# Sums of squares of two weight matrices: from Gram products on TensorE to squares on ScalarE

## The chip, the cores and the metric

The kernel runs on one core of one Trainium2 chip. The core has five engines with instruction streams of their own: PE (TensorE, matrix products), DVE (VectorE), ACT (ScalarE), POOL (GpSimd) and SP (SyncE, which issues the loads and stores here). What counts is the time of one execution in microseconds (us); the median of several runs is compared.

## The reference

Local and pooled attention feeds a mixing layer with an MLP (first block of weights), and then a gated layer. Cut to what matters here:

```python
def _moe_ref(x, w_ch1, w_ch2):               # x (4, 576, 512), w_ch1 (512, 2048), w_ch2 (2048, 512)
    X = np.fft.fft(np.fft.fft(x, axis=1), axis=2)
    u = x + np.real(X).astype(np.float32)
    mu = np.mean(u, axis=-1, keepdims=True)
    var = np.mean((u - mu) ** 2, axis=-1, keepdims=True)
    un = (u - mu) / np.sqrt(var + 1e-06)
    ch = np.maximum(un @ w_ch1, 0.0) @ w_ch2
    return (u + ch).astype(np.float32)

x = attention(q, k, v)                       # local window of 4, plus attention over means of 4
y = _moe_ref(x, w_ch1, w_ch2)
out = (sigmoid(conv5(y, conv_w)) * (y @ w_val)) @ w_out
```

## The kernel before

The inputs arrive as 64-bit floats. W1 (`w_ch1`, 512x2048) and W2 (`w_ch2`, 2048x512) are loaded as 32-bit halves of them, in eight tiles each, and DVE turns each tile of 128x1024 into float32 "words" by three instructions of `to_f32`: one shift (L302) and two instructions with two tensor inputs (L166, the helper `stt`). W1's tiles are taken in the order `W1_ORDER`; their places in that order are called positions 0 to 7. W2's tiles are 8 to 15.

The MLP works on 12 units of 192 positions, (b, j) for batch b and j = 0 to 2. Unit (0, 0) multiplies the float32 words themselves (`steps32`: the products `ph` with W1 at L1068, `pc` with W2 at L1081). This is the "coarse" unit. All other units multiply a float16 high and low part, in three passes (`mlp_steps`: `ph` at L1106, `pc` at L1126, with `hh` and `hl` the two parts of the hidden layer). For these "fine" units each weight tile is scaled by a power of two and split: `conv_w` lets ACT write the high part (L372) and DVE the low part (L166, float16 out). A tile's high part is put where the words of the tile before it stood, so the tiles of W1 are split one behind the other, ACT and DVE in turn.

The power of two comes from the sum of all squares of the matrix. `sumsq_w` forms it by Gram products: eight 128x128 bf16 products a tile (L356), 64 for W1 and 64 for W2, all added in one PSUM tile. `diagonal` multiplies this by the identity and reduces it (DVE), `total` adds over partitions with one more product (`tot`), ACT scales the result (`f2s_w1`, `f2s_w2`, L258), and `pow2` makes `s_w1` or `s_w2` and its inverse by four small instructions on POOL (L244 to L248). The split of W1 waits for `s_w1`, that of W2 for `s_w2`.

The norm in front of unit (b, j) is `ln`: mean, difference (`u32` for unit (0, 0), `uc` for the others), squares by ACT, their sum on PE (`st`), and an inverse root. For the units (0, 0) and (0, 1) the root is made on POOL by nine instructions on 128x192 (L1012, L169, L1019), with results `r00` and `r0`. `r00` is used only at the end of the coarse unit. `r0` is waited for by DVE's `uc<-uc,r` (L169), which the fine unit (0, 1) needs.

The order of the work is set by positions: `put` and `spread` give each step a number, the steps are emitted in the order of these numbers, `urgent` and `issue_after` (through the helper `behind`) add priorities and "not before" edges, and a scheduler then orders each engine's instructions. Loads stand in one chain on SP.

## Time and profile before

| what | value |
|---|---|
| median of 3 runs | 729.0 us (728.07 to 730.03) |
| the profiled execution | 730.66 us, of which the span is 728.9 us |
| PE busy | 687.0 us (94%) |
| DVE busy | 467.0 us (64%) |
| ACT busy | 316.9 us (43%) |
| POOL busy | 122.5 us (17%) |
| mean granted TensorE clock | 0.967 |

The span reaches from the first to the last instruction of the profiled execution; 1.7 us of its time lie outside it. A busy share over the whole span says little for one stretch: the stages have different limits, so the stretches around the change are read apart.

### The profile page before, as it was taken

Reading aid. Unit: us, or ns where it says so; the run is one execution under the profiler, and the core shown is the slowest. Engines: PE = TensorE matmul, PEld = TensorE weight load, DVE = VectorE, ACT = ScalarE, POOL = GpSimd, SP = SyncE. Lnnn points to the kernel's source line nnn. Section 1 sums busy time; section 2 is a strip of 40 time slices with the busy share of each in tenths; the row PEclk is TensorE's granted clock in tenths of the full one; section 3 lists DMA queues with packets and bytes.
Section 4 is the critical chain, followed back from the end, with each engine's and each line's share of the span. In section 5 each row is a group of like instructions: output and inputs, shape, how many; then the busy total and the mean of one; then the engine's idle time right before and its main releaser. Section 6 shows DMA issues by size and latency. Waiting matters only on the chain.

```text
span 728.9 us, 18440 instructions
## 1 busy us (share of the span) xinstructions
PE 687.0 (94%) x7849; PEld 599.6 (82%) x7849; DVE 467.0 (64%) x978; ACT 316.9 (43%) x980; POOL 122.5 (17%) x167
## 2 busy tenths in 40 slices
PE   8588799989899988999999999999999999999997
PEld 4346599988778967868898898789899989999895
DVE  4885699987978776466976725829635572633324
ACT  1674224686355336756423835644413232322212
POOL 0400054025222022330202107003100010000000
PEclk9758999989999999999999999999999999999999
DMA  9964314623422301240230001003000000000001
GB/s 240 377 228 167 101 66 167 155 82 129 144 60 83 100 1 39 61 136 16 77 103 2 26 15 43 17 1 97 18 16 16 1 16 16 1 17 2 30 2 44
DMA packets 27574, 53.01 MB, mean 73 GB/s; under 512 B 2112, under 2 KB 16320, under 8 KB 26468
## 3 DMA queue, kind: packets, MB, share of 16 engines
q1 hardware_dynamic: 27492, 51.84, 22.1%
q8 instruction: 61, 1.00, 0.6%
q14 instruction: 21, 0.17, 0.1%
HBM read 45.34 MB, written 8.26 MB: 74 GB/s over the span
## 4 chain that ended last, share of the span: by engine, by line
PE 67%; DVE 18%; ACT 6%; DMA 5%; POOL 2%; issue 1%; SPq 1%; POOLq 0%; ACTq 0%; DVEq 0%
PE pc L1126 19%; PE ph L1106 18%; DVE W L166 6%; PE out L1234 5%; PE val L1218 5%; ACT dP L565 3%; DMA v<-in_v_dram 2%; PE po L751 2%; PE ab L863 1%; DVE fF L835 1%; PE dO L606 1%; PE ph L1068 1%; DVE X L172 1%; PE sc L701 1%; PE pc L1081 1%
## 5 line engine op out<-in xcount | busy, mean ns | idle before, releaser
L1106 PE MATMUL ph<-uh,W 128*128 128x192 f16 x1408 | 195.3, 246 | 1.6 <-ACT uh L1032 1.6
L1106 PEld LDWEIGHTS <-W 128*128 128x128 f16 x2112 | 175.1, 98 | 7.9 <-issue 6.4
L1106 PE MATMUL ph<-ul,W 128*128 128x192 f16 x704 | 173.2, 246 | 0.0
L1126 PE MATMUL pc<-hh,W 128*128 128x192 f16 x1232 | 171.6, 247 | 0.9 <-ACT hh L1110 0.9
L1126 PEld LDWEIGHTS <-W 128*128 128x128 f16 x1848 | 154.2, 98 | 10.4 <-issue 8.4
L1126 PE MATMUL pc<-hl,W 128*128 128x192 f16 x616 | 151.3, 247 | 3.9 <-DVE hl L166 3.9
L166 DVE SCALAR_TENSOR_TENSOR hl<-ph,hh 128x384 f16<-128x384 f32 x88 | 48.2, 550 | 91.3 <-ACT hh L1110 91.2
L1110 ACT ACTIVATE hh<-ph 128x384 f16<-128x384 f32 x88 | 43.1, 494 | 103.0 <-PE ph L1106 99.9
L166 DVE SCALAR_TENSOR_TENSOR W<-X,cw,W 128x192 f32<-128x192 f32 x160 | 60.2, 432 | 0.9 <-ACT W L1181 0.7
L1218 PE MATMUL val<-yy,W 128*128 128x192 f16 x576 | 52.9, 246 | 0.1
L1218 PEld LDWEIGHTS <-W 128*128 128x128 f16 x576 | 47.9, 98 | 2.4 <-issue 0.6
L565 ACT ACTIVATE dP<-dS,dmx 128x64 f32<-128x64 f32 x160 | 48.1, 337 | 0.7 <-PE dPT L586 0.3
L1234 PE MATMUL out<-W,gh 128*128 128x512 f16 x144 | 45.6, 379 | 0.0
L565 ACT ACTIVATION_READ_ACCUMULATOR dP<-dS,dmx 128x1 f32 x160 | 36.8, 230 | 0.0
L166 DVE SCALAR_TENSOR_TENSOR W<-W,W 128x1024 int32<-128x1024 int32 x24 | 29.0, 1232 | 0.1
L715 ACT ACTIVATE E<-sc,nm 72x144 f32<-72x144 f32 x64 | 23.6, 378 | 9.4 <-POOL vr L172 4.7
L1234 PE MATMUL out<-W,gl 128*128 128x512 f16 x72 | 27.3, 379 | 0.0
L1081 PE MATMUL pc<-h,W 128*128 128x192 f32 x128 | 26.2, 357 | 0.0
L1234 PEld LDWEIGHTS <-gh 128*128 128x128 f16 x144 | 14.1, 98 | 13.7 <-issue 0.2
L1126 PE MATMUL pc<-hh,Wz 128*128 128x192 f16 x176 | 25.2, 246 | 0.0
L1068 PE MATMUL ph<-u,W 128*128 128x192 f32 x128 | 24.0, 345 | 1.0 <-DVE u L996 1.0
L1126 PEld LDWEIGHTS <-Wz 128*128 128x128 f16 x264 | 22.2, 98 | 2.7 <-issue 0.2
(243 smaller groups left out, 1208.1 us busy)
## 6 DMA issues: line engine op xcount, KB each, us to landing
W<-in_moe_w_ch_dram SPq DMA_DIRECT2D x12, 1024.0 KB
v<-in_v_dram SPq DMA_DIRECT2D x32, 144.0 KB
out_dram<-osb SPq DMA_DIRECT2D x17, 256.0 KB
vw<-in_v_dram SPq DMA_DIRECT2D x16, 256.0 KB
X<-in_q_dram SPq DMA_DIRECT2D x6, 576.0 KB
kT<-in_k_dram SPq DMA_DIRECT2D x4, 582.0 KB
X<-in_moe_w_ch_dram SPq DMA_DIRECT2D x2, 1024.0 KB
raw<-in_moe_w_ch_dram SPq DMA_DIRECT2D x4, 512.0 KB
```

Source lines behind the costliest of these rows:

```text
L166: return eng.scalar_tensor_tensor(out=out, in0=in0, scalar=scalar, in1=in1, op0=op0, op1=op1)
L172: return eng.tensor_tensor(out=out, in0=a, in1=b, op=ALU.add)
L565: A.activation(out=s_[:, z, a], in_=pss[par][:, z, a], func=AF.Exp, scale=SCALE, bias=mx[:, par, z, a:a + 1], accum_out=su[:, par, z, a:a ...
L715: A.activation(out=E[:, qc], in_=ps[:, qc], func=AF.Exp, scale=SCALE / 16, bias=nm[:, qc:qc + 1], accum_out=su[:, qc:qc + 1],)
L751: T.matmul(out=po[par * 64:par * 64 + 64], lhsT=d["vr"][:, kc, (a % 2) * 4 + (a // 2) * 2 + par], rhs=ets[par][:, kc], start=(kc == 0), st ...
L1068: i = T.matmul(out=ps[:, e], lhsT=W[AT[kc * 2 + m // 8] + 1][:, o:o + 128], rhs=u()[:, kc, :], start=(kc == 0), stop=(kc == 3))
L1081: T.matmul(out=c["ps"][m // 2][:, m % 2], lhsT=W[9 + g][:, o:o + 128], rhs=hs[g // 2][:, g % 2, e, :], start=(kk == 0 and m % 2 == 0), sto ...
L1106: T.matmul(out=ps[:, e], lhsT=w1_ap(pw, kc, 2 * g + e), rhs=uh[px][:, kc, :], start=(t == 0), stop=(t == 11))
L1110: A.activation(out=h_, in_=ps, func=AF.Relu)
L1126: T.matmul(out=ps[m // 2][:, m % 2], lhsT=w2_ap(pw, kk, m), rhs=x[px][:, e, :], start=(kk == 0 and (pw, px) == (0, 0) and m % 2 == 0), sto ...
L1218: T.matmul(out=ps[:, e], lhsT=wv_ap(pw, kc, 2 * mh + e), rhs=m_["y"][px][:, kc, :], start=(t == 0), stop=(t == 11))
L1234: T.matmul(out=ps, lhsT=(gh, gl)[px][:, kc, t * 128:(t + 1) * 128], rhs=wo_ap(pw, kc), start=(n == 0), stop=(n == 11))
```

## The change

Three things change. The sums of squares of W1 and W2 are made by ACT: one square of each 128x1024 tile with an accumulated sum, into one of eight columns, with the squares themselves thrown into a scratch tile (`Wz`). The Gram products and the diagonal go for these two (the third weight, `w_out`, keeps them), and `tot` now has eight columns, which ACT adds while it scales. The words of W1's tiles at positions 6 and 7 move from a place behind the first norm to the group of the other W1 tiles. The root of norm (0, 0) is emitted behind W1's scale, with an edge that keeps it there.

```diff
-S_W1B = -7.47
@@ pow2
         for dst, sg, z in ((s, 1.0, 0.0), (iv, -1.0, 254.0)):
-            eng.tensor_scalar(out=dst.bitcast(I32), in0=e, scalar1=sg * 2.0 ** 23, scalar2=z * 2.0 ** 23, op0=ALU.mult, op1=ALU.add)
+            last = eng.tensor_scalar(out=dst.bitcast(I32), in0=e, scalar1=sg * 2.0 ** 23, scalar2=z * 2.0 ** 23, op0=ALU.mult, op1=ALU.add)
+        if name == "w1":
+            st[0]["scaled"] = last
@@ total
         if act:
-            assert n == 1
             r = keep.tile([P, 1], F32, name="f2s_" + name)
-            A.activation(out=r, in_=ps, func=AF.Copy, scale=float(DM))
+            A.activation(out=tiny.tile([P, n], F32, tag="p2t", name="p2t"), in_=ps, func=AF.Copy, scale=float(DM), accum_out=r)
             return r
@@ word_w
-                       lambda g=gates if pos < 4 else gates1 if pos < 6 else gates2: g.pop(0) if len(g) > 1 else g[0])
-            if pos == 7:
-                gates2[:] = [last.ins]
+                       lambda g=gates if pos < 4 else gates1 if pos < 8 else gates2: g.pop(0) if len(g) > 1 else g[0])
@@ sumsq_w
+        if key != "wo":
+            if first:
+                gram[key] = keep.tile([P, 8], F32, name="ss_" + key)
+            behind(st[0]["sq"].ins if i < 8 else None, lambda: A.activation(
+                out=spare.bitcast(BF16)[:, 0:1024], in_=W[AT[i] + 1], func=AF.Square,
+                accum_out=gram[key][:, i % 8:i % 8 + 1]))
+            return
         if first:
-            gram[key] = pst("cv", [P, P]) if key == "wo" else ps_c.tile([P, P], F32, tag="c1", name="gram")
+            gram[key] = pst("cv", [P, P])
         x = W[AT[i] + 1].bitcast(BF16).rearrange("p (n t) -> p n t", t=2)
         for c in range(8):
             blk = x[:, c * 128:(c + 1) * 128, 1]
-            behind(st[0]["st2"].ins if i < 8 else None, lambda: T.matmul(
-                out=gram[key], lhsT=blk, rhs=blk, start=(first and c == 0), stop=(last and c == 7)))
+            T.matmul(out=gram[key], lhsT=blk, rhs=blk, start=(first and c == 0), stop=(last and c == 7))
@@ trace_w
-        return total(diagonal(gram[key], key), 1, key, key in ("w1", "w2"))
+        if key == "wo":
+            return total(diagonal(gram[key], key), 1, key)
+        return total(gram[key], 8, key, True)
@@ ln
+        def root():
+            behind(st[0]["scaled"].ins if head else None, lambda: e.tensor_scalar(out=r0.bitcast(I32), ...))
...
+        if head:
+            st[0]["r"], st[0]["root"] = r0, root
+            return
+        root()
@@ the positions
     put(S_G1[1], lambda: urgent(w1_scale, "S"))
+    put(S_G1[1], lambda: st[0]["root"]())
...
-    for r, f, p in ((W1_ORDER[:6], w_in, S_W1), ...
+    for r, f, p in ((W1_ORDER, w_in, S_W1), ...
-    for i in W1_ORDER[6:]:
-        put(S_W1B, lambda i=i: urgent(lambda: w_in(i), "S"))
```

The edits move instructions on all engines. Three places carry the prediction.

The first is POOL, at the two roots and W1's scale. `p2a`, `p2b`, `s_w1` and `iv_w1` are W1's scale, `r00` and one `r1` belong to the root of norm (0, 0), `r0` and the other `r1` to that of norm (0, 1). Before (the end of the second root; the whole first root and half of the second stand ahead of these rows):

```order
L169 TENSOR_TENSOR r1_1302<-r0_1300 128x192
L169 TENSOR_TENSOR r1_1302<-r1_1302,vv_1298 128x192
L244 TENSOR_SCALAR p2a_1207<-f2s_w1_1203 128x1
L1019 TENSOR_SCALAR r1_1302<-r1_1302 128x192
L246 TENSOR_SCALAR p2b_1209<-p2a_1207 128x1
L169 TENSOR_TENSOR r0_1300<-r0_1300,r1_1302 128x192
L248 TENSOR_SCALAR s_w1_1205<-p2b_1209 128x1
L248 TENSOR_SCALAR iv_w1_1206<-p2b_1209 128x1
```

Now:

```order
L243 TENSOR_SCALAR p2a_1139<-f2s_w1_1134 128x1
L245 TENSOR_SCALAR p2b_1141<-p2a_1139 128x1
L247 TENSOR_SCALAR s_w1_1137<-p2b_1141 128x1
L247 TENSOR_SCALAR iv_w1_1138<-p2b_1141 128x1
L1023 TENSOR_SCALAR r00_1083<-vv_1081 128x192
L168 TENSOR_TENSOR r1_1084<-r00_1083 128x192
L1023 TENSOR_SCALAR r0_1241<-vv_1239 128x192
L168 TENSOR_TENSOR r1_1084<-r1_1084,vv_1081 128x192
L168 TENSOR_TENSOR r1_1242<-r0_1241 128x192
L1029 TENSOR_SCALAR r1_1084<-r1_1084 128x192
...
L1029 TENSOR_SCALAR r1_1242<-r1_1242 128x192
L168 TENSOR_TENSOR r0_1241<-r0_1241,r1_1242 128x192
```

The scale stood behind 16 of the 18 instructions of the roots; now it stands ahead of all 18, the two roots alternate, and the last instruction of them is the one that DVE waits for.

The second place is ACT, from the square of the first norm to W1's scale and its first split. `Wz,ss_w1` and `Wz,ss_w2` are the new squares, `h32` the coarse unit's hidden layer, `vv` the norms' variances. Before:

```order
L1002 ACTIVATE sq_1068<-u32_1061 128x768
L1072 ACTIVATE h32_1213<-ph_1214 128x384
L1008 ACTIVATE vv_1075<-st_1070 128x192
L1002 ACTIVATE sq_1291<-uc_1284 128x768
...
L1008 ACTIVATE vv_1298<-st_1293 128x192
...
L258 ACTIVATE f2s_w1_1203<-tot_1201 128x1
L372 ACTIVATE W0_124<-W1_114,s_w1_1205 128x1024
```

Now:

```order
L1083 ACTIVATE h32_1154<-ph_1215 128x384
L352 ACTIVATE Wz_127,ss_w1_1123<-W7_117 128x1024
L1008 ACTIVATE sq_1232<-uc_1225 128x768
L352 ACTIVATE Wz_127,ss_w2_1341<-W9_118 128x1024
L1083 ACTIVATE h32_1257<-ph_1258 128x384
L352 ACTIVATE Wz_127,ss_w2_1341<-W9_118 128x1024
L352 ACTIVATE Wz_127,ss_w2_1341<-W11_119 128x1024
L258 ACTIVATE p2t_1135,f2s_w1_1134<-tot_1132 128x8
L352 ACTIVATE Wz_127,ss_w2_1341<-W11_119 128x1024
L1016 ACTIVATE vv_1239<-st_1234 128x192
L378 ACTIVATE W0_124<-W1_114,s_w1_1137 128x1024
```

All eight squares of W1 now stand between the square of norm (0, 0) and that of norm (0, 1), and three squares of W2 between the latter and W1's scale.

The third place is DVE, behind the difference of the first norm (`u32`). Before, there and at the place where DVE takes up the root's result:

```order
L996 TENSOR_TENSOR u32_1061<-X_132,st_1062 128x768
L302 TENSOR_SCALAR W7_117<-W13_120 128x1024
L302 TENSOR_SCALAR W7_117<-W15_121 128x1024
L166 SCALAR_TENSOR_TENSOR W7_117<-W13_120,W7_117 128x1024
...
L302 TENSOR_SCALAR W9_118<-W17_122 128x1024
L302 TENSOR_SCALAR W9_118<-W19_123 128x1024
...
L619 TENSOR_REDUCE qkT_805<-X_126 128x288 x2
L302 TENSOR_SCALAR W13_120<-W19_123 128x1024
L169 TENSOR_TENSOR uc_1284<-uc_1284,r0_1300 128x768
```

Now, at the same two places:

```order
L1002 TENSOR_TENSOR u32_1067<-X_132,st_1068 128x768
L302 TENSOR_SCALAR W9_118<-W17_122 128x1024
L302 TENSOR_SCALAR W9_118<-W19_123 128x1024
...
L625 TENSOR_REDUCE qkT_811<-X_126 128x288 x2
...
L165 SCALAR_TENSOR_TENSOR W13_120<-W19_123,W13_120 128x1024
L168 TENSOR_TENSOR uc_1225<-uc_1225,r0_1241 128x768
L165 SCALAR_TENSOR_TENSOR W13_120<-raw_1105,W13_120 128x512
...
L575 RECIPROCAL dsu_1197<-dsu_1197 128x8
L560 TENSOR_REDUCE dmx_1304<-dS_1268 128x8
```

The six instructions on `W7` have gone from here to the group that works on `W5`, in front of the first mixing steps. Between the reductions `qkT` and `uc<-uc,r0` stood one shift; now fifteen rows stand between them, and the `dmx` of the next attention group is still behind it.

## Rows read from the trace of the kernel before

**Rows 1.** Windows: stretch and its length, busy us of each engine, granted clock, DMA share, GB/s.

```profile
core 0: us, PE busy (x) PEld busy (x) DVE busy (x) ACT busy (x) POOL busy (x), PEclk, DMA share, GB/s
91.00:151.00 60.00, 59.43 (x621) 56.88 (x621) 59.22 (x83) 26.58 (x82) 20.59 (x28) 0.97 0.41 122
151.00:161.00 10.00, 7.80 (x47) 7.41 (x47) 7.77 (x10) 9.97 (x35) 0.00 (x0) 0.66 0.36 120
161.00:187.00 26.00, 21.87 (x312) 19.68 (x309) 21.34 (x39) 15.19 (x39) 13.99 (x13) 1.00 0.34 110
187.00:728.90 541.90, 527.86 (x6218) 472.32 (x6216) 320.78 (x734) 223.08 (x646) 77.79 (x105) 1.00 0.12 39
```

**Rows 2.** Chain of work that ended last, 90 to 187 us: start, length, what.

```profile
99.96 3.67 PE gram L356 x64
...
171.74 3.16 POOL vr L172
...
176.94 4.54 DMA raw<-in_moe_w_val_dram
```

**Rows 3.** Page, costliest groups: the attention's exponentials (busy, mean ns, idle before).

```profile
L565 ACT ACTIVATE dP<-dS,dmx 128x64 f32<-128x64 f32 x160 | 48.1, 337 | 0.7 <-PE dPT L586 0.3
```

**Rows 4.** Timeline of DVE, 90 to 135 us: start, busy, instruction, idle before.

```profile
91.38 1.29 DVE L302 TENSOR_SCALAR W<-W 128x1024 int32<-128x1024 int32 x2
92.58 4.62 DVE L166 SCALAR_TENSOR_TENSOR W<-W,W 128x1024 int32<-128x1024 int32 x4
...
109.62 1.10 DVE L302 TENSOR_SCALAR W<-W 128x1024 int32<-128x1024 int32 x1
...
113.37 5.12 DVE L619 TENSOR_REDUCE qkT<-X 128x288 f32<-128x1152 f32 x4
...
133.41 1.23 DVE L554 TENSOR_REDUCE dmx<-dS 128x8 f32<-128x512 f32 x2
```

**Rows 5.** Timeline of DVE, 50 to 66 us: the gap ahead of the mixing steps.

```profile
64.69 1.43 DVE L172 TENSOR_TENSOR X<-X,base 128x576 f32<-128x576 f32 x2 [8.67 <-ACT X L612]
```

**Rows 6.** Windows, the first 56 us.

```profile
0.00:56.00 56.00, 41.41 (x354) 23.45 (x355) 38.95 (x77) 30.39 (x155) 9.79 (x15) 0.74 0.85 282
```

**Rows 7.** Timeline of SP: the loads of W2's next tiles.

```profile
104.58 1.90 SPq L187 DMA_DIRECT2D W<-in_moe_w_ch_dram  x2
```

**Rows 8.** Timeline of ACT: the two scales, and the first split behind each.

```profile
111.98 0.17 ACT L258 ACTIVATE f2s_w<-tot 128x1 f32<-128x1 f32 x1
117.89 1.15 ACT L372 ACTIVATE W<-W,s_w 128x1024 f16<-128x1024 f32 x1 [5.74 <-POOL s_w L248]
...
150.53 1.15 ACT L372 ACTIVATE Wz<-W,s_w 128x1024 f16<-128x1024 f32 x1 [2.08 <-POOL s_w L248]
```

**Rows 9.** Timeline of ACT: a square with a sum of 128x1024 elsewhere in the kernel.

```profile
173.05 1.06 ACT L614 ACTIVATE vw<-vw 128x1024 f32<-128x1024 f32 x1
173.99 0.20 ACT L614 ACTIVATION_READ_ACCUMULATOR vw<-vw 128x1 f32 x1
```

**Rows 10.** Timeline of POOL: first, third, twelfth and sixteenth instruction of the two roots.

```profile
99.12 1.31 POOL L1012 TENSOR_SCALAR r<-vv 128x192 int32<-128x192 int32 x1 [17.63 <-ACT vv L1008]
...
101.10 3.91 POOL L169 TENSOR_TENSOR r<-r,vv 128x192 f32<-128x192 f32 x1
...
112.44 1.46 POOL L169 TENSOR_TENSOR r<-r,vv 128x192 f32<-128x192 f32 x1
...
115.67 0.59 POOL L169 TENSOR_TENSOR r<-r,vv 128x192 f32<-128x192 f32 x1
```

**Rows 11.** Timeline of PE, 103 to 167 us: coarse products, a gap, and the first fine `pc`.

```profile
103.47 3.47 PE L1068 MATMUL ph<-u,W 128*128 128x192 f32 x20
...
153.25 1.11 PE L606 MATMUL dO<-PT,vw 64*64 64x58 f32 x16 [2.20 <-ACT PT L592]
154.29 6.55 PE L1081 MATMUL pc<-h,W 128*128 128x192 f32 x22
...
166.47 0.25 PE L1126 MATMUL pc<-hh,Wz 128*128 128x192 f16 x1
```

More of the change, by code (lines that the diff above doesn't have):

```diff
@@ L1001, in ln @@
         sq = l_t("sq", [P, 4, UT])
-        A.activation(out=sq, in_=uc, func=AF.Square)
+        i = A.activation(out=sq, in_=uc, func=AF.Square)
+        if head:
+            st[0]["sq"] = i
         ps = colsum(sq, sq)
@@ L1011, in ln @@
         r0 = keep.tile([P, UT], F32, name="r00") if head else tiny.tile([P, UT], F32, tag="r0", name="r0", bufs=2)
-        e.tensor_scalar(out=r0.bitcast(I32), in0=vv.bitcast(I32), scalar1=-0.5, scalar2=float(0x5F1FFFF9),
-                        op0=ALU.mult, op1=ALU.add)
         r1 = tiny.tile([P, UT], F32, tag="r1", name="r1", bufs=2)
-        for a, c in ((-0.703952253, 0.703952253 * 2.38924456), (-0.5, 1.5)):
-            mul(e, r1, r0, r0)
-            if e is G:
-                mul(e, r1, r1, vv)
-                e.tensor_scalar(out=r1, in0=r1, scalar1=a, scalar2=c, op0=ALU.mult, op1=ALU.add)
-                mul(e, r0, r0, r1)
-            else:
-                stt(e, r1, r1, a, vv, ALU.mult, ALU.mult)
-                stt(e, r0, r1, c, r0, ALU.add, ALU.mult)
+        def root():
+            behind(st[0]["scaled"].ins if head else None, lambda: e.tensor_scalar(out=r0.bitcast(I32), in0=vv.bitcast(I32), scalar1=-0.5, scalar2=float(0x5F1FFFF9),
+                op0=ALU.mult, op1=ALU.add))
+            for a, c in ((-0.703952253, 0.703952253 * 2.38924456), (-0.5, 1.5)):
+                mul(e, r1, r0, r0)
+                if e is G:
+                    mul(e, r1, r1, vv)
+                    e.tensor_scalar(out=r1, in0=r1, scalar1=a, scalar2=c, op0=ALU.mult, op1=ALU.add)
+                    mul(e, r0, r0, r1)
+                else:
+                    stt(e, r1, r1, a, vv, ALU.mult, ALU.mult)
+                    stt(e, r0, r1, c, r0, ALU.add, ALU.mult)
+        if head:
+            st[0]["r"], st[0]["root"] = r0, root
+            return
+        root()
         r1 = r0
-        if head:
-            st[0]["r"] = r1
-            return
         mul(V, uc, uc, r1.unsqueeze(1).to_broadcast([P, 4, UT]))
@@ L1348, in attn_moe_kernel @@
         spread(steps, *p)
-    for r, f, p in ((W1_ORDER[:6], w_in, S_W1), (W1_ORDER[:4], w_out_, S_C0), (W1_ORDER[4:], w_out_, S_C1), (range(8, 16), w_in2, S_W2)):
+    for r, f, p in ((W1_ORDER, w_in, S_W1), (W1_ORDER[:4], w_out_, S_C0), (W1_ORDER[4:], w_out_, S_C1), (range(8, 16), w_in2, S_W2)):
         spread([(1.0, lambda i=i, f=f: urgent(lambda: f(i), "W")) for i in r], *p)
-    for i in W1_ORDER[6:]:
-        put(S_W1B, lambda i=i: urgent(lambda: w_in(i), "S"))
     for i in range(8, 16):
@@ L1361, in attn_moe_kernel @@
     assert S_LD[1] <= S_T0[0] and S_L1 <= S_W1[0] and S_T0[1] <= S_S0[0] and S_S0[1] <= S_F0[0] and S_F0[1] <= S_N0
-    assert S_N0 < S_W1B <= S_W2[0] and 4 / 17 < S_C0[0] and 8 / 17 < S_C1[0] and S_C1[1] <= 9 / 17
+    assert S_N0 <= S_W2[0] and 4 / 17 < S_C0[0] and 8 / 17 < S_C1[0] and S_C1[1] <= 9 / 17
     assert S_S0[1] <= S_END <= S_F0[0] and 1 <= S_W3[0]
```

## The prediction

> **What bounds the kernel now.** I read the windows first. Between 91 and 151 us, where the coarse unit runs and the weights are prepared, both PE (59.43 us) and DVE (59.22 us) are busy for the whole 60 us; ACT has 26.58 and POOL 20.59 [rows 1]. So two engines bound this stretch together, and work taken from only one of them would be worth little. From 151 to 187 us PE has holes: 2.2 us in the ten us behind 151, with the granted clock at 0.66 there, and 4.1 us up to 187. Behind 187 PE is busy for 527.86 of 541.90 us: the rest of the kernel is PE's, and whatever lead there is at 187 is carried to the end. The question is thus how much earlier the state of 187 us is reached.
>
> The chain of waits ends this stretch with an item that is not PE's: POOL's `vr` at 171.74, then the load of `w_val`, 4.54 us from 176.94 [rows 2], whose words DVE makes ahead of a low part `hl` that PE waits for. Both loads and `vr` hang on the attention of batch 1, that is on DVE's reductions `dmx`. The timeline of PE shows the hole of 2.20 us at 153.25, and behind it 22 coarse matmul pairs in 6.55 us, 0.30 each, where 20 took 3.47 us (0.17) at full clock [rows 11]. A hole on PE costs here about twice: itself, and the slower products behind it.
>
> **The Gram products.** The 64 of W1 hold the chain for 3.67 us [rows 2], so W1's and W2's together are 7.3 us of PE. It all lies in the bound stretch. PE gains from it only what DVE and ACT let it: the coarse products wait for words, and PE must turn over the attention's `dP`, which comes behind `dmx` on DVE. I count DVE's path, with PE's 7.3 us as the upper bound of a gain from this edit alone, and nothing as the lower.
>
> **The words.** The two tiles' six instructions stand on DVE from 91.38 to 97.12 us, 5.74 us [rows 4]. In the new order they go into the group in front of the mixing step, where DVE stands idle for 8.67 us until 64.69, waiting for ACT [rows 5]. They need their raw data there by about 56 us. In the first 56 us the DMA queues moved 282 GB/s, 15.8 MB [rows 6], and W1's eight tiles of 1.05 MB with the 4.9 MB ahead of them in the chain are 13.3 MB, so it has landed. 5.74 of 8.67 us: the words are hidden at no cost, with 2.9 us to spare. If the cover failed, 2.9 us or less of them would come back.
>
> So DVE leaves 91.4 us with W2's words at once. A second thing comes late by it: W2's tile 11. Its load was issued at 104.58 [rows 7], when the first words of W2 had freed its place, and used at 109.62 [rows 4], five us later. DVE now frees the place some 6.5 us earlier, at about 98.1, the load lands at 103.1, and DVE comes to it at 101.3: a wait of 1.8 us that was hidden before. The diagonal's multiplication and reduction also leave DVE, about 0.6 us as two small instructions. DVE without any other wait is thus 5.7 + 0.6 − 1.8 = 4.5 us earlier at `dmx` (133.41, [rows 4]).
>
> **The squares.** A square with a sum over 128x1024 took 1.06 us, and its sum's read ended 1.14 us behind its start [rows 9]. Sixteen are 18 us of ACT, which had 33 us idle in 91 to 151. The eight of W1 begin behind the first norm's square (about 92.4) and with `h32` and `vv` between them end at about 104; `sq` of norm (0, 1), three squares of W2 and a hidden layer follow, so `f2s_w1` comes at about 109 instead of 111.98, and as POOL's four small instructions are first in line, `s_w1` at about 110. Before, the first split began at 117.89, having waited 5.74 us for POOL [rows 8]. So W1's split is ready 8 us earlier, and ACT works it off earlier too.
>
> **The roots.** This is where the change pays. POOL used the time from 99.12 on for the roots, beside the wait for the sums; now all 18 instructions start at about 110.3. Their price depends on what DVE does: from 99.12 to 113.90 twelve took 14.8 us, 1.23 each, while DVE ran words, and a single one 3.91; under `qkT` one takes 0.59 [rows 10]. Both bounds: 18 × 0.59 = 10.6 us, end at 121; 18 × 1.23 = 22.2 us, end at 132.5. DVE takes up `r0` in `uc<-uc,r0`: `qkT` now runs from 106.7 to 111.7, and the fifteen rows behind it sum to 11 us by the durations of their kinds (four words of two inputs take 4.62), so DVE is there at about 122.8. Up to then POOL has done 2 instructions under `qkT`, some 4 in the 2.7 us of DVE's one-input rows, and 7 beside the 8.4 us of two-input rows: 13. The other 5 run while DVE stands still, at 0.6 each: DVE waits 3 us, until about 126. Everything behind `uc` on DVE waits with it, and `dmx` and `dP` of the next attention group are there.
>
> The Trainium skill says of this ("SBUF — State Buffer", section "SBUF: two separate sides") that a VectorE instruction with two SBUF inputs and a GpSimd instruction that reads SBUF take a shared port pair by an exclusive lock, and that the loser fully blocks. The trace's 3.91 us beside 0.59 agrees with it, and it speaks against moving POOL's root into DVE's words; taken strictly, it is the rival D below.
>
> **Behind `dmx`.** Of both signs: W2's diagonal, its reduction and waits are gone and a square is added, about −2; in ACT's new order the splits of W2 and sixteen exponentials (337 ns each, partly overlapping, [rows 3]) stand ahead of the first `hh` of unit (0, 1), as all its `ph` now come behind the coarse products, about +2 for the first fine `pc` (166.47, [rows 11]); the transposes of the second group, which PE had between, come earlier, about −1. Together −1, with bounds of −3 and +2.
>
> **The sum.** −4.5 + 3 − 1 = −2.5 us at 187, and PE carries it to the end. The profiled execution took 730.66 us, 1.7 above the median; the sum against it is 728.2, and against the median of 729.0, which I forecast, 726.5 us. A difference of 0.3%, 2.2 us, is about what this measurement can tell from none.
>
> **Rivals.**
> B: the root is in time (POOL near 0.59 an instruction, or `uc` reached late), and DVE and PE both gain. For it: the lower bound of 121 us lies ahead of DVE's 122.8. Then −4.5 − 1 = −5.5, and up to −7.3 where PE's own saving counts: 723.5 to 721.7 us; if the hole at 151 goes with it, down to 719.
> C: the lead at `dmx` is given back behind it. PE idles where it idled before, at 153 and up to 187, because `vr`, the load of `w_val` (4.54 us whatever the rest) and the first `hh` set it. For it: PE's 6.3 us of holes between 151 and 187 show that PE is not the limit there; against it: these loads hang on the same DVE chain, and come earlier with it. About 729.
> D, the other side: POOL is blocked by DVE's words all along and while waiting has no rest. At 1.23 us an instruction the root ends at 132.5, DVE waits 9.7 us, and −4.5 + 9.7 − 1 = +4.2: 733.2 us. It decides from a wait of about 5.5 us on, that is from a root that ends behind 128.3. Against it: while DVE waits for the root it runs nothing that could block POOL, so the last instructions are cheap.
> That the change doesn't do what it says is no rival: the Gram products and the rows of the words have moved in the new order.
>
> **Chances.** The forecast 0.42 (its own range 725 to 728; 0.27 of it faster by over 0.3%, 0.15 within), B 0.24, C 0.16, D 0.18. Faster 0.51, same 0.31, slower 0.18. The range reaches from 720 (most of B) to 732 (half of D): about 0.1 is left out on each side.
>
> **What would show it.** Right: no `gram` on PE for W1 and W2; two tiles' words between 56 and 62 us, and the next mixing step still at about 64.7; `s_w1` at about 110; POOL's last root instruction at 125 to 127, with DVE idle about 3 us ahead of `uc<-uc,r0`, released by POOL; `dmx` at about 132; the first PE hole at 151 smaller or 2 to 3 us earlier; a wait of about 2 us for the load of tile 11. Wrong: POOL's root ending behind 128 (D), or ahead of DVE (B); the mixing step later than 64.7, if the words are not covered; a lead at 133 that is gone at 187 (C); ACT late for `h32`, if PE waits for hidden layers behind the squares between 92 and 109.

## The result, and the profile after

The changed kernel takes 735.31 us (731.49 to 736.06, six executions), the kernel before on the same chip 728.16 us (727.64 to 730.03, six): a ratio of 1.0086, 95% interval 1.0063 to 1.011. It is slower by 7.1 us. The forecast was 726.5 us with a range of 720 to 732: wrong in sign, and outside the range. The profiled execution took 734.93 us, of which the span is 733.1.

The windows of the changed kernel, in the stretches of [rows 1]:

```profile
core 0: us, PE busy (x) PEld busy (x) DVE busy (x) ACT busy (x) POOL busy (x), PEclk, DMA share, GB/s
91.00:151.00 60.00, 55.97 (x533) 53.36 (x537) 54.32 (x67) 46.70 (x121) 18.74 (x28) 0.97 0.46 141
151.00:161.00 10.00, 8.53 (x98) 7.34 (x89) 7.75 (x13) 10.00 (x43) 2.27 (x3) 0.66 0.03 9
161.00:187.00 26.00, 20.42 (x268) 17.99 (x267) 24.46 (x50) 14.62 (x38) 11.04 (x10) 1.00 0.38 130
187.00:733.10 546.10, 529.12 (x6180) 471.76 (x6180) 321.86 (x725) 220.47 (x636) 81.75 (x105) 0.99 0.12 38
```

In the first row the change did what it says: PE and DVE are 3.5 and 4.9 us less busy, ACT 20 more. The rows up to 187 us have fixed ends, so the 4.2 us by which this span is longer must stand in the last row, which holds no edited instruction. I cut that row at the first fine `ph` of unit (1, 0). Before:

```profile
187.00:278.00 91.00, 85.07 (x976) 74.07 (x975) 72.60 (x167) 39.94 (x110) 17.23 (x24) 0.98 0.24 75
278.00:729.00 451.00, 442.79 (x5245) 398.25 (x5242) 248.19 (x568) 183.14 (x537) 60.55 (x81) 1.00 0.10 32
```

Changed:

```profile
187.00:281.00 94.00, 85.04 (x931) 71.20 (x932) 70.05 (x159) 38.39 (x115) 20.35 (x24) 0.95 0.20 64
281.00:733.10 452.10, 444.08 (x5251) 400.56 (x5248) 251.81 (x567) 182.07 (x522) 61.40 (x81) 1.00 0.10 33
```

The second part is 1.1 us longer; the first, with the same 85 us of PE, takes 94 instead of 91.

I then went down the path of batch 1 behind its attention, by the starts of five events: the reversal of half an image in DRAM (`dr<-dx`), the load of the result (`X<-dr`), the beginning of the norm of unit (1, 0) (`uc<-X` on DVE), the first fine `ph` of that unit on PE, and the end of the span. Two executions of either kernel (the second ones are experiments e13 and e15); every number is the start of a row of its timeline:

```
                              before  again   changed  again
dr<-dx issued (SP)            226.62  224.04  223.19   226.07
X<-dr issued (SP)             236.96  234.33  236.15   239.04
norm (1, 0) begins (DVE)      265.77  263.71  265.60   268.48
first fine ph of (1, 0) (PE)  277.62  275.68  280.77   283.65
end of the span               728.9   727.0   733.1    735.5
```

The times differ between executions by 3 us, the steps hardly. From `dr` to `X<-dr`: 10.34 and 10.29 before, 12.96 and 12.97 changed. From there to the norm: 28.81 and 29.38, 29.45 and 29.44. The norm's chain up to `ph`: 11.85 and 11.97 before, 15.17 twice changed. From `ph` to the end: 451.3 twice, and 452.3 and 451.9. By the means of the two executions the changed kernel is 0.7 us ahead at `dr`, loses 2.65 + 0.35 up to the norm, 3.26 in it, and 0.8 behind it: 6.4 us, which is the difference of the two spans' means.

These events are not PE's. PE's own time, up to `dr` and from there to the norm, before:

```profile
0.00:226.62 226.62, 198.79 (x2028) 160.67 (x2029) 177.25 (x326) 111.23 (x388) 52.00 (x70) 0.89 0.49 158
226.62:265.77 39.15, 37.78 (x454) 35.81 (x452) 30.52 (x65) 16.32 (x34) 7.11 (x12) 1.00 0.20 62
```

Changed:

```profile
0.00:223.19 223.19, 187.92 (x1866) 149.37 (x1867) 176.62 (x319) 128.26 (x422) 52.15 (x70) 0.89 0.49 160
223.19:265.60 42.41, 41.43 (x491) 38.77 (x488) 33.04 (x67) 16.26 (x34) 7.40 (x12) 1.00 0.18 57
```

Up to `dr` PE is idle for 27.83 us before and 35.27 changed (28.35 and 36.35 in the second executions): 7.7 us more in the mean, while the 128 Gram products are gone. From `dr` to the norm it is idle for 1.37 us before and 0.98 changed, though that step is 3 us longer: PE has 37 products more to do there. So `dr` now comes at an earlier point of PE's work, and a lead at `dr` is no lead in that work. When the norm begins, PE has begun 2351 products before and 2354 changed (Gram products not counted), and the changed kernel is there 2.3 us late in the mean of the two executions.

**The first loss.** The waits of SP for `X<-dr`, changed (who waited for what: us in total, times, longest):

```profile
SPq L856 <- DMA dr<-dx: 9.6, 1, 9.6
...
SPq L856 <- POOL fs L833: 2.6, 1, 2.6
```

Before, `X<-dr` waited for its transfer alone (9.6 us too). Now the transfer has landed, and it waits for POOL, whose difference `fs` still reads the part of X that the load overwrites. The timelines of POOL, before and changed:

```profile
229.20 1.92 POOL L827 TENSOR_TENSOR fs<-X 128x577 f32<-128x577 f32 x1 [6.12 <-DVE s_wo L248]
231.88 1.57 POOL L827 TENSOR_TENSOR fs<-X 128x577 f32<-128x577 f32 x1 [0.77 <-DVE ivvo L169]
```

```profile
229.85 2.37 POOL L833 TENSOR_TENSOR fs<-X 128x577 f32<-128x577 f32 x1 [9.66 <-DVE sof L165]
234.71 1.41 POOL L833 TENSOR_TENSOR fs<-X 128x577 f32<-128x577 f32 x1 [2.49 <-DVE FL L165]
```

The second ends at 236.12, and `X<-dr` is issued at 236.15. It waits for a buffer that DVE's low part `FL` gives back. DVE in the changed kernel, from the second of two splits of W_out on:

```profile
229.67 1.28 DVE L165 SCALAR_TENSOR_TENSOR W<-W,s_wo,W 128x1024 f16<-128x1024 f32 x1
230.87 1.97 DVE L165 SCALAR_TENSOR_TENSOR FL<-fF,s_x,FH 128x578 f16<-128x578 f32 x1
...
233.76 0.80 DVE L165 SCALAR_TENSOR_TENSOR FL<-fF,s_x,FH 128x578 f16<-128x578 f32 x1
```

Before, both `FL` come first (the second is shown) and the two splits of W_out follow:

```profile
230.72 1.01 DVE L166 SCALAR_TENSOR_TENSOR FL<-fF,s_x,FH 128x578 f16<-128x578 f32 x1
...
233.69 1.27 DVE L166 SCALAR_TENSOR_TENSOR W<-W,s_wo,W 128x1024 f16<-128x1024 f32 x1
```

The engines' orders are made anew with every build, and here one turned, 80 us behind the last instruction that was edited (W2's scale, whose first split stands at 144.87 us). That this costs time at the end is not shown by it: PE idles no longer here than before, as its own time above says.

**The second loss.** ACT at the norm of unit (1, 0), before:

```profile
268.39 0.84 ACT L1002 ACTIVATE sq<-uc 128x768 f32<-128x768 f32 x1 [5.34 <-DVE uc L996]
269.14 0.19 ACT L557 ACTIVATE dmx<-dmx 128x8 f32<-128x8 f32 x1
```

and changed:

```profile
267.65 0.21 ACT L563 ACTIVATE dmx<-dmx 128x8 f32<-128x8 f32 x1 [4.76 <-DVE dmx L560]
...
270.22 0.88 ACT L1008 ACTIVATE sq<-uc 128x768 f32<-128x768 f32 x1
```

The scaling `dmx` and eight exponentials of batch 2 now stand ahead of the square, on which everything hangs: `st`, the root, `uh`, and the unit's products. PE runs out of work meanwhile. Its timeline there, changed:

```profile
269.24 0.38 PE L539 MATMUL dS<-bandb 128*128 128x512 bf16 x1 [1.63 <-ACT dP L571]
...
272.81 0.98 PE L996 MATMUL st<-sq,ones 128*128 128x192 f32 x2 [1.19 <-DVE sq L171]
...
274.35 0.61 PE L1245 MATMUL out<-W,gh 128*128 128x512 f16 x1
```

Before, the same `st` stands at 270.55 and takes 0.56 us, and an `out` product 0.38: behind these holes the clock is the lower one, 1.2 GHz, in the changed kernel. The windows say it too, changed:

```profile
265.00:272.00 7.00, 3.67 (x94) 2.33 (x91) 5.19 (x11) 3.41 (x18) 1.29 (x3) 0.98 0.01 2
272.00:278.00 6.00, 5.19 (x27) 2.34 (x28) 4.69 (x9) 0.92 (x6) 2.04 (x3) 0.50 0.00 0
```

where before's second row has 1.00. So two theories: (T1) the loss is the turned orders, and undoing an order returns its part; (T2) one of the three edits costs by itself (the squares on ACT, say, or the late root), and the orders are a by-product; and as a third (T3), the lower clock is the cost. In the expectations below, theory 3 is the late root, which here is a part of T2, and T3 stands there as the second half of theory 1.

### The profile page after: what moved, and what is told of

It is laid out like the page before. It is cut to its first block, busy times and chain, and to the rows that moved or that the text cites. A ratio compares the mean times of both kernels' runs of the same rounds, so it can differ in the third digit from the quotient of the medians.

```text
span 733.1 us, 18217 instructions
## 1 busy us (share of the span) xinstructions
PE 683.5 (93%) x7721; PEld 593.5 (81%) x7721; DVE 472.8 (64%) x974; ACT 333.8 (46%) x1014; POOL 124.0 (17%) x167
## 5 line engine op out<-in xcount | busy, mean ns | idle before, releaser
L1117 PE MATMUL ph<-uh,W 128*128 128x192 f16 x1408 | 199.3, 249 | 0.6 <-ACT uh L1043 0.6
L1117 PE MATMUL ph<-ul,W 128*128 128x192 f16 x704 | 175.1, 249 | 0.7 <-DVE ul L1044 0.7
L165 DVE SCALAR_TENSOR_TENSOR W<-X,cw,W 128x192 f32<-128x192 f32 x160 | 62.8, 448 | 0.6 <-ACT W L1192 0.4
L1245 PE MATMUL out<-W,gh 128*128 128x512 f16 x144 | 47.2, 391 | 0.0
L707 PE MATMUL sc<-qkT 64*72 64x144 f32 x128 | 21.0, 326 | 3.6 <-ACT E L721 1.7
```

The source lines that it names most:

```text
L165: return eng.scalar_tensor_tensor(out=out, in0=in0, scalar=scalar, in1=in1, op0=op0, op1=op1)
L707: T.matmul(out=pss[par][:, qc], lhsT=d["qkT"][r, 0, a, qc * QC:(qc + 1) * QC], rhs=d["qkT"][r, 1, a, :], start=True, stop=True,)
L1117: T.matmul(out=ps[:, e], lhsT=w1_ap(pw, kc, 2 * g + e), rhs=uh[px][:, kc, :], start=(t == 0), stop=(t == 11))
L1245: T.matmul(out=ps, lhsT=(gh, gl)[px][:, kc, t * 128:(t + 1) * 128], rhs=wo_ap(pw, kc), start=(n == 0), stop=(n == 11))
```

## The experiments

All but the two second looks were timed in rounds against the kernel before on the same chip (medians 728.1 to 729.0 there). The groups ran on different chips, so kernels of different groups are compared by their ratios to it. None leaves out a part of the reference's computation.

### One edit at a time: e1, e2, e3, e4

e1 makes only the squares, e2 only the words, e3 only the late root, e4 squares and words with the root at its old place.

Against before, e1, e2 and e3 in this order:

```diff
+            behind(st[0]["sq"].ins if i < 8 else None, lambda: A.activation(
+                out=spare.bitcast(BF16)[:, 0:1024], in_=W[AT[i] + 1], func=AF.Square, ...
```

```diff
-    for r, f, p in ((W1_ORDER[:6], w_in, S_W1), ...
+    for r, f, p in ((W1_ORDER, w_in, S_W1), ...
```

```diff
+    put(S_G1[1], lambda: st[0]["root"]())
```

e4 against the changed kernel:

```diff
-    put(S_G1[1], lambda: st[0]["root"]())
```

> Before with the squares on ScalarE alone: words and root where they were. Theory 1 (the 7.3 us of Gram products are given back as waits on PE ahead of 187 us, and the loss of some 4 us comes from the stretch of 260 to 290 us, where the squares of the norm of unit (1, 0) now stand behind eight to sixteen exponentials on ScalarE): the order of ScalarE is turned there too, so 731 to 735 us. Theory 2 (the loss comes from what the edits do themselves between 91 and 187 us, through ScalarE's 18 us of squares): 733 to 737. Theory 3 (the root behind the scale costs the time): the root is as before, so 726 to 729.

> Before with the words of W1's tiles 6 and 7 in the first part alone; Gram products and root as they were. Theory 1: the 5.7 us go from VectorE into an idle stretch, but the order of ScalarE is turned at unit (1, 0) here too (the square behind twelve exponentials), so no better than before, 728 to 733 us. Theory 2: nothing of the squares is here, so the words' gain stays, 724 to 727 us. Theory 3: the same, 724 to 727.

> Before with the first norm's root behind W1's scale alone; Gram products and words as they were. Theory 1: the scale comes only some 2 us earlier, the root is late for VectorE by 5 us or more, and ScalarE's order is turned at unit (1, 0) too: 731 to 737 us. Theory 2: about 729. Theory 3: 733 to 737, nearly all of the loss.

> The changed kernel with the first norm's root at its old place; every other instruction stands in the changed kernel's order (TensorE's order is the same instruction for instruction). Theory 1: the wait for the root was half a us, and the late stretch is as in the changed kernel: 733 to 736 us. Theory 2: the same, 733 to 736. Theory 3: 726 to 729.

Measured: e1 735.92 us, 1.0107 [1.0075, 1.0138]; e2 731.33, 1.004 [1.0024, 1.0056]; e3 741.2, 1.0164 [1.0132, 1.0196]; e4 732.7, 1.0053 [1.0034, 1.0073]. No theory foretold all four: e1 lies above theory 1's range and in theory 2's, e2 in theory 1's alone, e3 above every range, e4 just below those of theories 1 and 2. No sum of effects explains them: e1 and e2 would make 11 us together and make 4.4, and the root that costs 13 us alone costs 2.6 in company. That speaks against T2 as a plain sum and for something that flips. The norm's chain flips: 14.55, 15.46, 14.79 and 15.17 us in e1 to e4, by the same two events as in the table. The first loss is in none of the single edits (`X<-dr` comes 10.1 to 10.2 us behind `dr` in e1 to e3), and in e4 it is (12.96).

### The order alone: e5, and back: e6, e7, e8

e5 is the kernel before with one order turned by hand, in the norm of unit (1, 0); its orders are before's until about 265 us.

```diff
-        A.activation(out=sq, in_=uc, func=AF.Square)
+        behind(st[2]["exp", 0].ins if (b, j) == (1, 0) else None, lambda: A.activation(out=sq, ...))
```

e6, e7 and e8 turn it the other way in the changed kernel, in e3 and in e1; for that the norm is also emitted at an earlier position, `P_L`.

```diff
-P_L = {1: 2.1, 2: 4.9, 3: 8.5}
+P_L = {1: 1.99, 2: 4.9, 3: 8.5}
-                A.activation(out=mx, in_=mx, func=AF.Copy, scale=-SCALE)
+                behind(st[1]["lsq"].ins if b == 2 and g == 0 else None, lambda: A.activation(out=mx, ...))
```

> The kernel before with one edge: the square of the norm of unit (1, 0) on ScalarE comes behind the eight exponentials per half of the next attention group. Up to that place, at about 265 us, every engine's order is that of before; none of the change's edits is in it. Theory 1 (the loss comes from this order, in the stretch of 260 to 290 us): 731.5 to 733.5 us. Theory 2 (the loss comes from the edits' own work between 91 and 187 us, and the late stretch only passes it on): 727.5 to 729.

> The changed kernel with one edge the other way: the next group's maximum and exponentials on ScalarE come behind the square of the norm of unit (1, 0), as in the kernel before. Theory 1: the loss behind 260 us is gone, and the 0.4 us of lead there is left: 727 to 729.5 us. Theory 2: 733 to 736, as without the edge.

> The root behind the scale alone (the slowest of the single edits, 741 us), with the same edge. Theory 1: most of its loss lies behind 260 us, where it had a lead of 2.5 us: 725 to 730 us. Theory 2: 737 to 741.

> The squares on ScalarE alone, with the same edge. Theory 1: its lead of 1.8 us at 260 us is left: 725 to 729 us. Theory 2: 733 to 736.

Measured: e5 735.03 us, 1.0086 [1.0052, 1.0119]; e6 731.81, 1.0043 [1.0026, 1.0059]; e7 730.98, 1.0028 [1.0009, 1.0047]; e8 738.06, 1.0131 [1.0103, 1.016]. One turned order, with no edit of the change in the kernel, costs 6.5 us, nearly as much as the whole loss. Up to 268 us every engine's order in e5 is before's; behind it PE's and DVE's orders turn too. ACT in e5:

```profile
268.87 0.21 ACT L557 ACTIVATE dmx<-dmx 128x8 f32<-128x8 f32 x1 [6.00 <-DVE dmx L554]
...
271.44 0.88 ACT L1002 ACTIVATE sq<-uc 128x768 f32<-128x768 f32 x1
```

Its norm begins at 265.58, as before's, and its `ph` stands at 282.17: a chain of 16.59 us, 1.4 longer than the changed kernel's, so e5 costs more than this place costs there. Turned back, the chain is 13.11 in e6 and 13.12 in e7, not before's 11.9, and 3.5 and 10.2 us come back, 3.1 and 9.9 by the ratios (6.3 of the 10.2 behind `ph`, where e3 had 457.7 us left and e7 has 451.3). Both end above the range of theory 1 and below that of theory 2. e8 is a miss, above both: its chain is 14.91, and its norm begins only at 270.69, as `dr` is issued at 230.82, 3.8 us later than in e1, whose orders are the same up to 268 us. PE waits longer on the way; in e1 this wait is 0.3 us:

```profile
PE eT L749 <- POOL E L169: 2.9, 1, 2.9
```

The `E` that PE waits for there took POOL 3.95 us, in e1 0.95 us; the part on the prediction comes back to it. So for the squares alone one order was not the cause, and what it is was not settled.

### The clock: e9, e10

Into e6 and e7 go 14 idle products of 128x512 on PE behind the first sum of that norm, so that PE does not stand still; nothing reads them.

```diff
-            T.matmul(out=ps, lhsT=ones, rhs=t[:, 0], start=True, stop=True)
+            m = T.matmul(out=ps, lhsT=ones, rhs=t[:, 0], start=True, stop=True)
+            if (b, j) == (1, 0) and src is x:
+                warm_after(m, 14)
```

> The changed kernel with the square of the norm of unit (1, 0) kept in front (as in the pinned one), and with 14 idle products of 128x512 on TensorE between the two sums of that norm, where TensorE stood idle for 3.4 us and the granted clock then fell to 0.5 for 6.8 us. Their results are not read. If what is left of the loss there is the clock (theory 1, second half): the fall goes, some 3 us are won against the pinned kernel's 731.8: 727.5 to 730. If the clock costs nothing there because TensorE waits anyway: 731 to 733.

> The root behind the scale alone, pinned, with the same 14 idle products. It came to 260 us with the best lead of all, 3.2 us, and lost it by a hole of 5.3 us and a fall of the clock. Theory 1: 726 to 729 us against 731 without the products. If the clock costs nothing there: 730 to 732.

Measured: e9 732.17 us, 1.0039 [1.0015, 1.0063]; e10 731.62, 1.0032 [1.0014, 1.005]. The windows of e9 in the same two stretches:

```profile
265.00:272.00 7.00, 6.49 (x77) 4.35 (x75) 6.06 (x12) 1.29 (x5) 1.66 (x2) 1.00 0.01 2
272.00:278.00 6.00, 5.49 (x87) 3.22 (x86) 5.01 (x13) 3.65 (x17) 2.89 (x4) 1.00 0.10 37
```

The lower clock is gone (e6 had 0.79 and 0.68 in these rows), the chain is 0.6 us shorter than in e6, and the time is the same. So T3 falls for e6: in that stretch PE waits for the chain whatever its clock. e10 says less: its clock still falls for 3.4 us there (0.76 in the first row), its chain is 13.66 us for 13.12 in e7, and its time is e7's. The products were not put into the changed kernel as it is.

### Words, Gram products and root, each with the order turned back: e11, e12, e14

e11 is e2 with e6's edit. e12 is e6 with all 128 Gram products back on PE, into a tile that nobody reads. e14 is e6 with the root at its old place; PE's order is the same in both.

The edits of e12 and of e14:

```diff
+            blk = x[:, c * 128:(c + 1) * 128, 1]
+            behind(st[0]["st2"].ins if i < 8 else None, lambda: T.matmul(
+                out=gram[key, 0], lhsT=blk, rhs=blk, start=(first and c == 0), stop=(last and c == 7)))
```

```diff
-    put(S_G1[1], lambda: st[0]["root"]())
```

> The words alone (731.3 us), with the square of the norm of unit (1, 0) kept in front of the exponentials, of which twelve of sixteen stood ahead of it. Theory 1: its lead of 0.5 us at 260 us is left: 727 to 729.5. Theory 2: 730.5 to 732.

> The changed kernel, pinned, with all 128 Gram products back on TensorE; nobody reads them, the squares of ScalarE are used. This puts 7.3 us of TensorE's work back between 100 and 150 us. If TensorE waits for the others ahead of 187 us anyway (theory 1, first half: the removed products were worth nothing): 730 to 733 us, as without them. If they were worth their length: 737 to 740.

> The changed kernel with the root of norm (0, 0) at its old place, pinned at the norm of unit (1, 0). TensorE's order is that of the pinned changed kernel, instruction for instruction. If the late root is what is left of the loss (theory 3 in part): 728 to 730 us. If not: 731 to 733.

Measured: e11 727.99 us, 0.9993 [0.9976, 1.001]; e12 732.33, 1.0046 [1.0029, 1.0064]; e14 729.73, 1.0012 [0.9993, 1.0031]. The words alone cost nothing and bring nothing; the 3 us of e2 were the order. The Gram products make no difference at the end, though they do on the way: with them PE waits, among others,

```profile
PE gram L360 <- DVE W L165: 4.5, 1, 4.5
```

and `dr` comes at 227.01 instead of 223.52. But e12's order has `X<-dr` 10.05 us behind it, and 449.8 from `ph` to the end: what the products cost, other places of its order give. So the value of the edit by itself cannot be read from this pair. The late root costs 2.1 us (e6 over e14; 2.3 by the ratios, whose intervals still overlap), of which the next pair shows the place.

### Second looks: e13, e15

e13 is the kernel before and e15 the changed one, unedited, profiled again.

> The kernel before once more, for a second profile: 727 to 731 us. If its executions differ by TensorE's clock, the falls of the clock lie at other places or are fewer than in the first profile (6.8 us from 153 and 3.4 us from 187); if they differ by waits, the clock's falls are the same.

> The changed kernel once more, for a second profile: 731 to 737 us. By theory 1 TensorE's clock falls again between 265 and 290 us, behind the holes of the norm of unit (1, 0), in most executions; if the first profile was a rare one there, it does not.

Measured: 728.81 and 737.23 us. They are the two columns "again" of the table. One kernel's own executions differ by 2.6 to 2.9 us at `dr`, so that a lead of 3.4 us in one pair of profiles (226.62 against 223.19) proves little; the steps from `dr` on repeat to 0.6 us at most, most of them to 0.1. In e15 the clock falls again behind the norm's holes, from 271.5 us for 10.2 us; in e13 it falls at 268.8 and not at 187, so the places of the falls differ between executions of before.

### The first loss turned back as well: e16, e17

e16 is e14, e17 is e6, both with the splits of W_out and the diagonals behind `FH` and `FL`, as before has them. PE's order is the same in both, and they differ by the root's place alone.

```diff
+        wo = i >= 18
-        A.activation(out=h_, in_=r_, func=AF.Copy, scale=s[:, 0:1])
+        behind(st[1]["mh", 0, 1].ins if wo else None, lambda: A.activation(out=h_, in_=r_, ...))
-            stt(eng, l_, r_, s[:, 0:1], h_, ALU.mult, ALU.subtract)
+            behind(st[1]["ml", 0, 1].ins if wo else None, lambda: stt(eng, l_, r_, ...))
```

> The kernel with squares and words, the root at its old place and the order at norm (1, 0) turned back, with a second order turned back: ScalarE's and VectorE's splits of W_out and the diagonals of the convolution stand behind the high and low parts of the first two mixing pieces of batch 1, as they do in the kernel before. Theory: in the changed order the load of the mirrored half (X<-dr) waits for GpSimd's last difference fs, 12.96 us behind the issue of dr<-dx, where the kernel before loads it after 10.3 us; so 2.65 us of any lead are lost there. Turned back, X<-dr is issued 10.3 us behind dr (dr at about 221, X<-dr at about 231.3), norm (1, 0) begins 29.4 us behind that, and its chain takes 12 to 13.6 us: the first fine ph of that unit at about 273.5 and the end 451.3 to 452.8 us behind it, a median near 727 instead of 729.7, ratio about 0.998. Rival: the later work, whose order turns too, gives it back: no lead at the first ph, or a longer rest behind it than 453 us, and 729.7 or more.

> The changed kernel with both orders turned back; it differs from the run beside it by the late root alone, with TensorE's order the same. Theory: X<-dr 10.3 us behind dr here too, 2.65 us won against the changed kernel with one order turned back (731.8), so about 729; the late root keeps its 2 us above the kernel with the early root. Rival one: the loss at X<-dr was not on the path and the time stays at 731 to 732. Rival two: the root's 2 us belonged to the order and not to the root, and both kernels of this pair are equal.

Measured: e16 728.59 us, 1.0005 [0.9989, 1.002]; e17 731.21, 1.0043 [1.0024, 1.0062]. By the ratios e16 is 0.5 us below its twin e14, and e17 is level with e6; the intervals separate neither. That is what rival one said for e17: the loss at `X<-dr` was not on the path. `X<-dr` follows `dr` by 11.1 us instead of 12.96, as SP waits 0.9 us for POOL instead of 2.6, but from there to the norm it is now 31.0 instead of 29.4: most of the gain was given back at once. e16 issues `dr` at 220.09, 4.0 and 6.5 us ahead of before's two profiles, and its median is before's: at `dr` PE has begun 1866 products, where before had begun 1900 and 1893 without the Gram ones.

The pair shows the root cleanly. DVE in e17, and in e16 the same instruction:

```profile
119.49 1.61 DVE L165 SCALAR_TENSOR_TENSOR W<-W,W 128x1024 int32<-128x1024 int32 x1
...
126.43 0.96 DVE L168 TENSOR_TENSOR uc<-uc,r 128x768 f32<-128x768 f32 x1 [2.35 <-POOL r L168]
```

```profile
120.34 0.95 DVE L169 TENSOR_TENSOR uc<-uc,r 128x768 f32<-128x768 f32 x1
121.21 1.21 DVE L166 SCALAR_TENSOR_TENSOR W<-W,W 128x1024 int32<-128x1024 int32 x1
```

e17 is 1.7 us ahead at the words and 2.6 us behind after `uc<-uc,r`. Behind it DVE stays 2.6 us late (`dmx` at 131.89 against 129.26), and PE at 134 us waits in e17 for what hangs on it, in e16 not at all:

```profile
PE dPT L594 <- DVE dP L168: 2.6, 1, 2.6
```

`dr` is 2.56 late, and the median 2.62; here the intervals do not overlap. By the ratios the loss is thus 0.86% in the changed kernel, 0.43% with the order at the norm turned back (e6), and 0.12% with the root at its old place as well (e14), which is not clear of zero.

## Why the prediction was wrong, by its own steps

**"What bounds the kernel now"** is the step that failed, in its last sentence: "Behind 187 PE is busy for 527.86 of 541.90 us: the rest of the kernel is PE's, and whatever lead there is at 187 is carried to the end." It is carried only from the first fine `ph` of unit (1, 0) on, at 277 us: from there 449.8 to 452.8 us are left in 18 of the 19 profiles (e3 has 457.7). What the runs show in its place: up to `dr` PE has given back in idle time all that the Gram products freed; the late root costs 2.6 us (e16, e17), about what the sum had for it; and the norm's chain, which the sum did not have, costs 3.26 us more, by an order that turned (e5, e6).

A busy share of 97% over 542 us (527.86 of 541.90) is made of 93% up to 278 us (85.07 of 91) and 98% behind. Of the 5.9 idle us up to there, 4.6 stand at the norm of unit (1, 0). In the changed kernel PE is idle for 9.0 us up to its `ph`: 5.3 at that norm, and 2.6 at 190 to 192 us, where before had none up to 205. Of these 2.6, 2.2 are a wait for POOL's `E` in batch 1's pooled attention (2.2 again in the second execution; before had 0 and 1.0). POOL and DVE there, changed (of three long DVE instructions the first and the last):

```profile
189.57 2.81 POOL L168 TENSOR_TENSOR E<-E,lsu 72x288 f32<-72x288 f32 x1 [10.75 <-DVE lsu L726]
```

```profile
189.65 0.68 DVE L165 SCALAR_TENSOR_TENSOR W<-raw,W 128x512 int32<-128x512 int32 x1
...
190.91 0.94 DVE L168 TENSOR_TENSOR uc<-uc,r 128x768 f32<-128x768 f32 x1
```

Up to 223 us e17 has the orders of e6 on every engine (but for two pairs of neighbours on PE). In e6 this `E` took 2.82 us, and PE waited for it as in the changed kernel; in e17, where DVE stood idle beside it, it took 0.66, and PE did not wait:

```profile
190.48 0.66 POOL L168 TENSOR_TENSOR E<-E,lsu 72x288 f32<-72x288 f32 x1 [10.42 <-PE po L759]
```

So here a wait of 2.2 us comes and goes with the moment at which `E` begins, the orders being equal. How much of the 2.3 us at the norm's beginning it accounts for was not tested. Rival C ("the lead at `dmx` is given back") came nearest: the holes that it named are there, 7.05 idle us from 151 to 187 against 6.33. But it ended at 729.

**What no rival had**: that the order of work turns at two places, 223 to 236 and 267 to 270 us, where nothing was edited. The steps there are 2.65 and 3.26 us longer. That the second costs time is shown by e5 and e6. Of the first only the wait is shown: PE had other work there, and turning the order back returned 0.5 us (e16) and nothing (e17). I compared the orders at the edited places and not there.

**The Gram products.** Between nothing and 7.3 us was right as bounds, and the lower one came: up to `dr` PE is idle for 7.7 us more. Its longest waits from 125 to 200 us, changed:

```profile
PE pc L1137 <- DVE hl L165: 2.5, 2, 2.0
PE eT L747 <- POOL E L168: 2.2, 1, 2.2
PE dPT L592 <- DVE dP L168: 1.9, 1, 1.9
```

With seven shorter ones they are 13.7 us, where the same view of before has 6.4. The time became waits for DVE, ACT and POOL, as "PE gains from it only what DVE and ACT let it" said; which edit each wait comes from the list does not tell.

**The words.** Right: the eight two-input words stand at 52.23 in one run, and the mixing comes no later:

```profile
52.23 9.16 DVE L165 SCALAR_TENSOR_TENSOR W<-W,W 128x1024 int32<-128x1024 int32 x8
64.16 2.10 DVE L171 TENSOR_TENSOR X<-X,base 128x576 f32<-128x576 f32 x3 [2.77 <-ACT X L618]
...
102.30 0.69 DVE L302 TENSOR_SCALAR W<-W 128x1024 int32<-128x1024 int32 x1 [1.69 <-DMA W<-in_moe_w_ch_dram]
```

`X<-X,base` was at 64.69 [rows 5]. The wait for tile 11 is 1.69 us, forecast 1.8.

**The squares.** Right: 1.04 to 1.06 us each and 0.18 to 0.20 for the sum's read; `s_w1` is there at 108.6, forecast 110.

**The roots.** Right in size: the last instruction ends at 124.96 us, forecast 126, and the late root costs 2.1 to 2.6 us in all, forecast 3. But in the profiled execution DVE waits 0.48 us and not 3, and pays the rest in slower words: the rows of 128x1024 with two inputs took 1.41, 1.61 and 1.36 us beside POOL, 1.21 without it. POOL in its turn took 0.89 us an instruction (18 in 16.0 us). In e17 the wait is 2.35 us. Each of the two waits for whole instructions of the other:

```profile
119.58 1.02 POOL L168 TENSOR_TENSOR r<-r,vv 128x192 f32<-128x192 f32 x1
120.57 1.57 POOL L168 TENSOR_TENSOR r<-r,r 128x192 f32<-128x192 f32 x1
```

```profile
120.08 1.61 DVE L165 SCALAR_TENSOR_TENSOR W<-W,W 128x1024 int32<-128x1024 int32 x1
```

The word ends at 121.69, 1.09 us behind the end of POOL's first row (alone it takes 1.21), and POOL's second row ends 0.45 us behind the word (alone it takes 0.59). The rule cited from the Trainium skill ("SBUF — State Buffer", section "SBUF: two separate sides"), that the loser of the lock fully blocks, agrees with these rows. D's 22.2 us became 16.0: POOL got a turn behind nearly every word, and four of the 18 instructions ran under `qkT`, at 0.35 to 0.59 us, where the prediction counted two. The prediction took DVE's one-input rows as cheap for POOL; but one took 1.05 us beside POOL, 0.69 without it.

**Behind `dmx`, and the sum.** `dmx` is at 130.45, 3.0 us earlier than in [rows 4] (forecast 1.5), and the first fine `pc` at 161.78, 4.7 us earlier than in [rows 11]; but in the second execution they are at 134.04 and 165.45. Five profiles with the late root's order (changed twice, e6, e9, e17) against three with before's order up to there (before twice, e5) give leads of 1.8 us at `dmx`, 3.5 at the first fine `pc`, and 1.5 at `dr` (224.05 against 225.54, where the groups spread over 3.4 and 2.6 us). The sum, −2.5, was thus right in sign up to the first fine `pc`. The 1.5 us at `dr` are a lead by the time alone, as PE has done less by then.

**What stays open**: the loss of the squares alone (e1, e8); how much time POOL's `E` costs, as no run changes that place alone; why e3 takes 6 us more behind `ph` than the others (its PE waits 3.2 us for ACT's `E` at 300 to 320 us, which e7 does not); and what the change would bring with before's orders at both places, which no kernel here reaches.

## What to carry to other kernels

A high busy share over a long stretch doesn't say that a lead is carried through it: look for chains in it that are not the busy engine's (here a norm with one square in it), because time won ahead of such a chain can be lost there. Judge a lead by the busy engine's own work: here a transfer was issued earlier, with less of PE's work done, and the lead was none. Where instruction orders are made anew with every build, compare them over the whole program, and test an edit also with the order pinned: here one turned order moved the time by 6.5 us in the kernel before and by 3 in the changed one, and the late root by 2 to 2.6. One pair of profiles carries the scatter of two executions; the distances between fixed events repeat far better than the times, and show where a difference arises.

## What was not expected of the hardware

DVE and POOL wait for each other by whole instructions, and the wait can be many times the instruction's own time. In e16 a DVE instruction on one element in each partition, 0.15 us elsewhere, took 1.37 and ended with POOL's `fs`, at 227.41 and 227.39:

```profile
225.56 1.83 POOL L834 TENSOR_TENSOR fs<-X 128x577 f32<-128x577 f32 x1 [8.46 <-DVE fF L842]
```

```profile
226.04 1.37 DVE L166 SCALAR_TENSOR_TENSOR sof<-iv_y,ivvo 128x1 f32<-128x1 f32 x1
```

The low part `FL` of 1.97 us in the changed kernel (0.80 elsewhere) ends 0.62 us behind its `fs`. POOL can lose several times in a row: the root's row of 3.91 us [rows 10] ends behind four words of DVE that are no slower than alone, and `E` in the changed kernel behind three instructions. And the same program, run again, meets the lower clock at other places: before at 187.1 to 190.6 us in one profile and at 268.8 to 272.2 in the other. Its `dr` is 2.6 us later in the first; whether by the clock was not tested.
